# A three-stage kernel on one core: the filler's Silu made from tanh, and Silu's table loaded ahead

## The chip, the core and the metric

The kernel runs on one core of a Trainium2 chip. The metric is the device time of one execution in microseconds; less is better. A core has TensorE (matmuls, which read SBUF and write PSUM), ScalarE (activation functions from tables, copies), VectorE and GpSimd (elementwise work; GpSimd here works on SBUF only), and queues that start DMA transfers, here SyncE's. Each engine works through its own instructions in program order and waits for the others by semaphores. ScalarE has one table of functions active at a time; the profile shows a change of table as an instruction of its own, ACT_TABLE_LOAD.

## The reference

Three computations follow each other, all in float32. The notation below is the reference's, cut to what is computed:

```
scores = q @ k.T / 8 - slope[head] * distance      # causal, window of 128 keys, 576 tokens
x = softmax(scores) @ v                            # 4 batches x 8 heads, joined to x [2304, 512]
g = x @ w_gate                                     # [2304, 1536]
y = (g * sigmoid(g) * (x @ w_val)) @ w_out         # [2304, 512]
h = y @ w_in2                                      # [2304, 2048]
out = (h * cos(h)) @ w_out2                        # [2304, 512]
```

The product `g * sigmoid(g)` is Silu of g.

## The kernel before, in words

Every float32 matmul is made of three: each operand is split into a high part (rounded) and a low part (the rest), and high x high, high x low and low x high are summed in PSUM (`mm3`, lines 79 to 82). Much of the other engines' work is this splitting: a copy or cast to the high part, a subtraction for the low part.

**The attention phase** (lines 690 to 764) runs 144 items, nine for each of 16 pairs of batch and head pair. It is a software pipeline written out by hand: one turn `n` of the loop issues the scores of an item ahead, the bias (VectorE, line 540), Exp (ScalarE, line 549), the sum's reciprocal (VectorE, lines 555 and 560), the normalization (GpSimd, line 565), the transposes (TensorE, line 575), the copy of a transposed tile to its high part (ScalarE, line 592), the low part (VectorE, line 601), and the product with v (TensorE, line 638), each for an item some turns older than the one before. A list `post` carries work to the next turn: at its start a turn takes the whole list (line 703), and runs it behind its own issues and ahead of the filler (line 727). What a listed function appends to `post` runs one turn later. A second list, `pool_bg`, holds GpSimd work, of which each turn issues a bounded part.

**The filler.** TensorE's free time in that phase is filled with the second computation for the first three of its twelve column blocks (F0 = 3, 128 columns each). A generator (`filler`, line 284) walks over eight jobs, the two halves of 288 tokens of each of the four batches, as soon as the batch's attention is done. A job has 12 steps of the gate's matmuls (`a_l1` with "g": three column blocks by four parts of the inner dimension), then the 12 steps of the job before's second matmul (`a_l2`), then 12 steps of the value's matmuls (`a_l1` with "v"). Each step is one `mm3` of 288 columns. A turn adds 1.6 steps to what is due (RATE, lines 690, 696 and 730), and line 764 caps what may be carried over at the same 1.6, so that steps missed in a long wait are not made up within the phase. What is left of the filler runs after it (line 1037).

When a gate block is done, `evac_l1` (line 230) is called by way of `post`. It copies the block from PSUM to its third of the tile `fu` on ScalarE (line 234). With the third block it applies Silu to the whole tile of 128x864 (line 236) and sets a flag, `st["silu"]`. The filler holds the value's matmuls back until that flag is there (line 219):

```
while (nm, f) not in g0 or (nm == "v" and "silu" not in st):
    yield "wait"
```

The evacuation of a value block multiplies it with `fu` on VectorE (line 243); GpSimd then splits the product into `fh` and `fl` (lines 244 and 247), the operands of the second matmul. `fu` has one buffer, so the first copy of a job waits for the last `fl` of the job before.

**After the filler** line 1053 issues the first gate and value matmuls of the second computation's other blocks, and then the last job's second matmul (`a_l2`), whose four blocks VectorE and ScalarE evacuate in turn (lines 267 and 269). The rest of the second computation (`begin`, line 940) uses Silu at line 946, and the third, from about 640 us, uses Sin at line 1155 for the cosine, with VectorE's line 1152 in the chain before it. All these stages consist of matmuls in an order that is fixed in the program.

Of the kernel before, what the change touches and what calls it, by code (L numbers as in the profile page):

```python
# [9 lines left out]
F32 = mybir.dt.float32  # L10
F32R = mybir.dt.float32r
U32 = mybir.dt.uint32
AF = mybir.ActivationFunctionType
ALU = mybir.AluOpType
# [14 lines left out]
def kernel(  # L29
# [12 lines left out]
    nc = tc.nc  # L42
# [8 lines left out]
    HT = S // 2  # L51
# [8 lines left out]
    persist = ctx.enter_context(tc.tile_pool(name="persist", bufs=1))  # L60
    dram = ctx.enter_context(tc.tile_pool(name="dram", bufs=1, space=DRAM))
    halfpi = persist.tile([128, 1], F32, name="halfpi")
    xs, cv = ExitStack(), ExitStack()
    x_pool = xs.enter_context(tc.tile_pool(name="xhl", bufs=1, reuse_waits="tile"))
    wa2_p = ctx.enter_context(tc.tile_pool(name="wa2", bufs=3, side="right", reuse_waits="tile"))
# [10 lines left out]
    def f32(ap):  # L76
        return ap.bitcast(F32)

    def mm3(ps, ah, al, bh, bl, start, stop):
        nc.tensor.matmul(out=ps, lhsT=ah, rhs=bh, start=start, stop=False)  # L80
        nc.tensor.matmul(out=ps, lhsT=ah, rhs=bl, start=False, stop=False)  # L81
        nc.tensor.matmul(out=ps, lhsT=al, rhs=bh, start=False, stop=stop)  # L82
# [89 lines left out]
    post = deque()  # L172
# [10 lines left out]
    F0 = 3  # L183
    g0 = {}
    fa = ExitStack()
    pm = ctx.enter_context(tc.tile_pool(name="pm", bufs=2, space=PSUM, side="right"))
    fill_p = fa.enter_context(tc.tile_pool(name="fill", bufs=1, side="right"))
    ye_p = fa.enter_context(tc.tile_pool(name="ye", bufs=4, side="right"))

    g0_todo = []  # L190
    pools0 = [wa_p, wa_p, wa2_p]
# [5 lines left out]
    def flush():  # L197
        for _ in range(len(post)):
            post.popleft()()
# [9 lines left out]
    def bank():  # L209
        turn[0] += 1  # L210
        if more and turn[0] % 3 == 0:
            return more[0].tile([128, 512], F32, tag="l1", name="l1")
        return pm.tile([128, 512], F32, tag="pm", name="pm")

    def a_l1(job, nm, fs, st):
        b, hf = job
        tok = slice(b * S + hf * HT, b * S + (hf + 1) * HT)
        for f in fs:
            while (nm, f) not in g0 or (nm == "v" and "silu" not in st):
                yield "wait"  # L220
            ps = bank()
            wh, wl = g0[nm, f]
            for kk in range(KD):
                c = slice(kk * 128, (kk + 1) * 128)
                mm3(ps[:, :HT], wh[:, c], wl[:, c], xh[:, kk, tok], xl[:, kk, tok], kk == 0, kk == KD - 1)
                if kk == KD - 1:
                    post.append(lambda ps=ps, f=f: evac_l1(nm, f, st, ps))
                yield

    def evac_l1(nm, f, st, ps):  # L230
        if nm == "g":
            if f == 0:
                st["u"] = fill_p.tile([128, F0, HT], F32, tag="fu", name="fu")
            nc.scalar.copy(out=st["u"][:, f], in_=ps[:, :HT])
            if f == F0 - 1:
                nc.scalar.activation(out=st["u"], in_=st["u"], func=AF.Silu)
                st["silu"] = True
            return
        if f == 0:
            st["h"] = fill_p.tile([128, F0, HT], F32R, tag="fh", name="fh")  # L240
            st["l"] = fill_p.tile([128, F0, HT], F32R, tag="fl", name="fl")
        u, hi, lo = st["u"][:, f], st["h"][:, f], st["l"][:, f]
        nc.vector.tensor_tensor(out=u, in0=u, in1=ps[:, :HT], op=ALU.mult)  # L243
        pool_bg.append((0.35, lambda: nc.gpsimd.tensor_scalar(hi, u, 1.0, 0.0, ALU.mult, ALU.add)))

        def low():
            nc.gpsimd.tensor_tensor(out=lo, in0=u, in1=f32(hi), op=ALU.subtract)
            if f == F0 - 1:
                st["ready"] = True
        pool_bg.append((0.7, low))  # L250

    def a_l2(job, st):
        b, hf = job
        t0 = b * S + hf * HT
        while "ready" not in st or ("o", F0 - 1) not in g0:
            yield "wait"
        for e in range(KD):
            ps = bank()
            for f in range(F0):
                wh, wl = g0["o", f]  # L260
                c = slice(e * 128, (e + 1) * 128)
                mm3(ps[:, :HT], wh[:, c], wl[:, c], st["h"][:, f], st["l"][:, f], f == 0, f == F0 - 1)
                if f == F0 - 1:
                    def ev(ps=ps, e=e):
                        y = ye_p.tile([128, HT], F32, tag="ye", name="ye")
                        if e % 2:
                            nc.vector.tensor_copy(out=y, in_=ps[:, :HT])
                        else:
                            nc.scalar.copy(out=y, in_=ps[:, :HT])
                        nc.sync.dma_start(out=y1d[e, :, t0:t0 + HT], in_=y)  # L270
                    post.append(ev)
                yield
# [110 lines left out]
    for j in range(2):  # L383
        pair = []
        for nm in ("h", "l"):
            t = const.tile([128, 128], F32R, name=f"qt{nm}{j}")
# [3 lines left out]
        t = const.tile([128, 128], F32, name=f"qt{j}")  # L390
# [13 lines left out]
    for j in range(2):  # L404
        t = big.tile([128, NB, 4, D], F32, tag=f"vhl{j}", name=f"vx{j}")
# [289 lines left out]
    for n in range(N + PVS + 2):  # L695
        due += 0.7 * RATE
        u, idx = divmod(n, NI)
# [230 lines left out]
    def l1_mms(w, t0, n, ps=None):  # L928
        if ps is None:
            ps = bank()  # L930
        wh, wl = w
        tok = slice(t0, t0 + n)
        for kk in range(KD):
            c = slice(kk * 128, (kk + 1) * 128)
            mm3(ps[:, :n], wh[:, c], wl[:, c], xh[:, kk, tok], xl[:, kk, tok], kk == 0, kk == KD - 1)
        return ps[:, :n]
# [114 lines left out]
    load_acc(0)  # L1051
    i, tb, f = steps[0]
    early = [l1_mms(weights[i, nm, f], *tbs[tb], pl2.tile([128, 512], F32, tag="l2", name="l2")) for nm in ("v", "g")]
    for _ in a_l2(*last[0]):
        flush()
    flush()
# [22 lines left out]
    for k in range(K + 1):  # L1079
        if k < K:  # L1080
            i, tb, f = steps[k]
# [34 lines left out]
    def new_bank(n):  # L1116

        if n < 12 and n % 3:
            return pl2.tile([128, 512], F32, tag="l2", name="l2")
        return pm.tile([128, 512], F32, tag="pm", name="pm")  # L1120
# [118 lines left out]
    for k in range(K2 + 2):  # L1239
# [3 lines left out]
        for m in range(7):  # L1243
            if k < K2:
                if k == 0 and m < 2:
                    ps = bank0[m]
                elif m == 6:
                    prod(k, m, p7, start=False)
                    ps = p7
                else:  # L1250
                    ps = new_bank(7 * k + m)
# [57 lines left out]
```

## Time and profile before

| | us |
|---|---|
| median of 3 runs | 1018.39 |
| lowest and highest run | 1017.4, 1020.55 |
| the profiled execution, its own time | 1020.49 |
| its span, first to last instruction | 1018.3 |
| mean granted clock of TensorE, as a share of 2.4 GHz | 0.988 |
| attention phase with filler, without its thin start | 84 to 250 us of the span |
| the filler's rest | 250 to 300 us |

The profile lists for each engine the time in which it was busy. A group of instructions is named by its line, engine, operation and tiles (written <- read); then come the count, the busy time in us, the mean of one in ns, and the idle time of the engine just before them with what ended it. TensorE's matmuls are pipelined, so that the duration of one is longer than the distance of two starts.

### The profile page before, as it was taken

How to read it: one execution, taken by the hardware profiler on the slowest of the kernel's cores; microseconds unless marked ns; L12 is line 12 of the kernel's file. 1: busy time of each engine (PE TensorE's matmuls, PEld its weight loads, DVE VectorE, ACT ScalarE, POOL GpSimd, SP SyncE). 2: the span in 40 equal slices, each digit the busy share in tenths (PEclk: the TensorE clock that was granted, in tenths of full speed). 3: DMA queues.
4: the chain of work that ended last, by engine and by line, in shares of the span. 5: the costliest groups of instructions: out<-in, count | busy, mean ns of one | idle time of the engine just before them, and what ended most of it. 6: DMA issues, size and time to landing. Idle time of an engine off the chain costs nothing.

```text
span 1018.3 us, 17545 instructions
## 1 busy us (share of the span) xinstructions
PE 977.8 (96%) x5796; PEld 914.2 (90%) x5796; DVE 758.4 (74%) x1588; ACT 637.2 (63%) x1426; POOL 506.7 (50%) x575
## 2 busy tenths in 40 slices
PE   5779999999999999999999999999999999999998
PEld 3558999889999999999999999888999998989986
DVE  5996787776419898998989945789766797656664
ACT  5887888877215454555555532787767777677663
POOL 4775576665315666866867850234323343222231
PEclk9888999999999999999999999999999999999999
DMA  6551243212256454755846651856758566575552
GB/s 155 135 130 37 61 104 83 74 45 69 65 177 222 137 184 128 248 162 162 267 125 203 217 168 71 327 181 196 235 189 261 163 197 201 166 259 175 184 184 82
DMA packets 145161, 163.67 MB, mean 161 GB/s; under 512 B 64688, under 2 KB 105648, under 8 KB 144816
## 3 DMA queue, kind: packets, MB, share of 16 engines
q1 hardware_dynamic: 145072, 162.57, 51.4%
q8 instruction: 46, 0.75, 0.3%
q14 instruction: 43, 0.35, 0.1%
HBM read 126.88 MB, written 35.65 MB: 160 GB/s over the span
## 4 chain that ended last, share of the span: by engine, by line
PE 83%; ACT 7%; DVE 5%; issue 2%; DMA 2%; SPq 1%; POOL 0%; ACTq 0%; DVEq 0%; POOLq 0%
PE l L80 13%; PE l L81 13%; PE l L82 13%; PE pm L80 7%; PE pm L82 7%; PE pm L81 7%; PE pm L1033 5%; PE pm L1034 5%; PE pm L1035 5%; PE s L532 3%; PE t L575 2%; PE pv L638 2%; DVE e L540 1%; DVE ct L125 1%; PE pq L417 1%
## 5 line engine op out<-in xcount | busy, mean ns | idle before, releaser
L1157 POOL TENSOR_TENSOR r<-r,c 128x384 f32<-128x384 f32 x96 | 104.3, 1088 | 260.2 <-ACT r L1155 167.5
L80 PE MATMUL pm<-xh,wh 128*128 128x384 f32 (+1 forms) x452 | 152.3, 337 | 0.4 <-DVE fu L243 0.4
L82 PE MATMUL pm<-xh,wl 128*128 128x384 f32 (+1 forms) x452 | 145.9, 323 | 0.0
L81 PE MATMUL pm<-xl,wh 128*128 128x384 f32 (+1 forms) x452 | 145.9, 323 | 0.0
L81 PE MATMUL l<-wo,hh 128*128 128x512 f32 x288 | 113.1, 393 | 0.0
L80 PE MATMUL l<-wo,hh 128*128 128x512 f32 x288 | 113.0, 393 | 0.0
L82 PE MATMUL l<-wo,hl 128*128 128x512 f32 x288 | 112.9, 392 | 0.0
L854 POOL TENSOR_TENSOR cs<-cs,st 128x512 uint32<-128x512 uint32 x56 | 80.4, 1436 | 57.5 <-DVE cs L852 49.2
L1033 PE MATMUL pm<-xh,ws 128*128 128x384 f32 x318 | 107.4, 338 | 0.6 <-ACT q L1183 0.6
L1035 PE MATMUL pm<-xh,ws 128*128 128x384 f32 x318 | 107.1, 337 | 0.0
L1034 PE MATMUL pm<-xl,ws 128*128 128x384 f32 x318 | 107.1, 337 | 0.0
L565 POOL TENSOR_SCALAR e<-e,st 128x256 f32<-128x256 f32 (+1 forms) x144 | 67.0, 475 | 71.3 <-DVE st L560 27.1
L80 PEld LDWEIGHTS pm<-xh,wh 128*128 128x128 f32 x452 | 86.1, 190 | 1.9 <-DVE fu L243 0.7
L81 PEld LDWEIGHTS pm<-xl,wh 128*128 128x128 f32 x452 | 86.0, 190 | 0.0
L82 PEld LDWEIGHTS pm<-xh,wl 128*128 128x128 f32 x452 | 85.8, 190 | 0.0
L1147 ACT ACTIVATE a<-c 128x384 f32<-128x384 f32 x96 | 49.7, 518 | 53.6 <-DVE c L1173 53.6
L1152 DVE SCALAR_TENSOR_TENSOR r<-a,r 128x384 f32<-128x384 f32 x96 | 76.1, 793 | 3.3
L1154 ACT ACTIVATE r<-r 128x384 f32<-128x384 f32 x96 | 50.3, 524 | 41.7 <-DVE r L1152 41.7
L80 PE MATMUL l<-uh,wh 128*128 128x384 f32 x216 | 72.8, 337 | 0.0
L82 PE MATMUL l<-uh,wl 128*128 128x384 f32 x216 | 72.7, 337 | 0.0
L81 PE MATMUL l<-ul,wh 128*128 128x384 f32 x216 | 72.7, 336 | 0.0
L955 ACT CAST uh<-s 128x384 fp32r<-128x384 f32 x54 | 27.7, 514 | 69.9 <-PE l L82 62.2
(196 smaller groups left out, 2863.4 us busy)
## 6 DMA issues: line engine op xcount, KB each, us to landing
ws<-wid SPq DMA_DIRECT2D x168, 256.0 KB, 2.8
wo<-wod SPq DMA_DIRECT2D x48, 512.0 KB, 4.8
st<-in_moe_w_out_dram SPq DMA_DIRECT2D x28, 512.0 KB, 3.7
st<-in_moe_w_in_dram SPq DMA_DIRECT2D x16, 512.0 KB, 3.8
st<-in_moe_w_gate_dram SPq DMA_DIRECT2D x12, 512.0 KB, 4.2
st<-in_moe_w_val_dram SPq DMA_DIRECT2D x12, 512.0 KB, 3.7
wid<-sh SPq DMA_DIRECT2D x24, 256.0 KB, 4.0
wid<-sl SPq DMA_DIRECT2D x24, 256.0 KB, 3.6
```

Source lines behind the costliest of these rows:

```text
L80: nc.tensor.matmul(out=ps, lhsT=ah, rhs=bh, start=start, stop=False)
L81: nc.tensor.matmul(out=ps, lhsT=ah, rhs=bl, start=False, stop=False)
L82: nc.tensor.matmul(out=ps, lhsT=al, rhs=bh, start=False, stop=stop)
L565: nc.gpsimd.tensor_scalar(e[:, :w], e[:, :w], st[:, 6 + m:7 + m], 1.0, ALU.mult, ALU.mult)
L854: nc.gpsimd.tensor_tensor(out=ti, in0=ti, in1=st[:, :, 0], op=ALU.add)
L1033: nc.tensor.matmul(out=o, lhsT=wh, rhs=xh_, start=start and kk == 0, stop=False, skip_group_check=True)
L1034: nc.tensor.matmul(out=o, lhsT=wh, rhs=xl_, start=False, stop=False, skip_group_check=True)
L1035: nc.tensor.matmul(out=o, lhsT=wl, rhs=xh_, start=False, stop=kk == 1, skip_group_check=True)
L1147: nc.scalar.activation(out=a, in_=h, func=AF.Copy, scale=INV2PI, bias=MAGIC)
L1152: nc.vector.scalar_tensor_tensor(out=r, in0=a, scalar=-C2, in1=r, op0=ALU.mult, op1=ALU.add)
L1154: nc.scalar.activation(out=r, in_=r, func=AF.Abs)
L1157: nc.gpsimd.tensor_tensor(out=r, in0=r, in1=h, op=ALU.mult)
```

## The change

In the filler the gate's Silu is made in another way. With u = g / 2, g * sigmoid(g) = (tanh(u) + 1) * u. For each gate block ScalarE copies the bank with a scale of 0.5 into `fu`; one turn later it makes tanh of that into a new tile `th` (two buffers); one turn after the tanh VectorE makes (t + 1) * u in place, in one scalar_tensor_tensor. The flag is set with the third block's last operation. Besides, a Silu of one column into a tile that nobody reads stands behind the first matmuls of the next stage, ahead of the last job's second matmul.

```diff
@@ -60,6 +60,7 @@
     halfpi = persist.tile([128, 1], F32, name="halfpi")
+    gone = persist.tile([128, 1], F32, name="gone")
@@ -186,6 +187,7 @@
     ye_p = fa.enter_context(tc.tile_pool(name="ye", bufs=4, side="right"))
+    th_p = fa.enter_context(tc.tile_pool(name="th", bufs=2, side="right"))
@@ -231,10 +233,17 @@
         if nm == "g":
             if f == 0:
                 st["u"] = fill_p.tile([128, F0, HT], F32, tag="fu", name="fu")
-            nc.scalar.copy(out=st["u"][:, f], in_=ps[:, :HT])
-            if f == F0 - 1:
-                nc.scalar.activation(out=st["u"], in_=st["u"], func=AF.Silu)
-                st["silu"] = True
+
+            u = st["u"][:, f]
+            nc.scalar.activation(out=u, in_=ps[:, :HT], func=AF.Copy, scale=0.5)
+            t = th_p.tile([128, HT], F32, tag="th", name="th")
+            post.append(lambda: nc.scalar.activation(out=t, in_=u, func=AF.Tanh))
+
+            def gate():
+                nc.vector.scalar_tensor_tensor(out=u, in0=t, scalar=1.0, in1=u, op0=ALU.add, op1=ALU.mult)
+                if f == F0 - 1:
+                    st["silu"] = True
+            post.append(lambda: post.append(gate))
             return
@@ -1051,6 +1060,7 @@
     early = [l1_mms(weights[i, nm, f], *tbs[tb], pl2.tile([128, 512], F32, tag="l2", name="l2")) for nm in ("v", "g")]
+    nc.scalar.activation(out=gone, in_=halfpi, func=AF.Silu)
     for _ in a_l2(*last[0]):
```

## Rows read from the trace of the kernel before

**Rows 1.** The page: busy us of each engine, share of the span, instructions.

```profile
PE 977.8 (96%) x5796; PEld 914.2 (90%) x5796; DVE 758.4 (74%) x1588; ACT 637.2 (63%) x1426; POOL 506.7 (50%) x575
```

**Rows 2.** Busy times by stage; columns us, busy us (instructions) by engine, PEclk, DMA.

```profile
84.00:250.00 166.00, 156.15 (x1285) 147.18 (x1285) 124.26 (x461) 134.85 (x383) 108.05 (x207) 0.98 0.29 72
250.00:300.00 50.00, 49.81 (x364) 49.36 (x363) 16.03 (x31) 14.06 (x27) 11.80 (x18) 1.00 0.27 90
```

**Rows 3.** Groups of ScalarE instructions, whole span.

```profile
L1155 ACT ACTIVATE r<-r,halfpi 128x384 f32<-128x384 f32 x96 | 59.3, 618 | 3.1
...
L946 ACT ACTIVATE s<-pm 128x384 f32<-128x384 f32 x35 | 17.2, 492 | 49.1 <-PE pm L82 49.1
...
L234 ACT COPY fu<-pm 128x288 f32<-128x288 f32 x22 | 8.6, 395 | 13.7 <-POOL fl L247 11.0 <-PE pm L82 2.7
...
L236 ACT ACT_TABLE_LOAD x6 | 7.7, 1283 | 0.1
L236 ACT ACTIVATE fu<-fu 128x864 f32<-128x864 f32 x8 | 7.4, 926 | 0.1
...
L549 ACT ACT_TABLE_LOAD x5 | 6.4, 1283 | 0.1
...
L678 ACT ACT_TABLE_LOAD x1 | 1.3, 1283 | 0.7 <-PEq L1293 0.7
```

**Rows 4.** Timeline of ScalarE, first half's Silu; columns start us, duration us.

```profile
88.65 1.28 ACT L236 ACT_TABLE_LOAD   x1
89.95 0.93 ACT L236 ACTIVATE fu<-fu 128x864 f32<-128x864 f32 x1
90.89 1.28 ACT L549 ACT_TABLE_LOAD   x1
```

**Rows 5.** Busy times by stage, five stretches around the pairs of table loads.

```profile
88.00:100.00 12.00, 9.90 (x75) 8.72 (x74) 7.73 (x28) 10.64 (x26) 6.02 (x12) 0.86 0.15 33
114.00:124.00 10.00, 8.53 (x72) 8.08 (x72) 6.30 (x21) 9.84 (x26) 4.04 (x9) 1.00 0.05 16
150.00:158.00 8.00, 7.13 (x63) 6.44 (x63) 4.09 (x18) 7.70 (x18) 4.44 (x9) 1.00 0.16 37
186.00:198.00 12.00, 9.59 (x79) 8.68 (x78) 6.71 (x24) 11.12 (x27) 3.85 (x9) 1.00 0.37 89
224.00:232.00 8.00, 6.60 (x58) 5.97 (x56) 4.46 (x19) 7.88 (x20) 4.61 (x10) 1.00 0.20 52
```

**Rows 6.** Timeline of TensorE; in brackets idle us before, and its releaser.

```profile
93.22 0.29 PE L81 MATMUL pm<-xl,wh 128*128 128x288 f32 x1
93.35 0.29 PE L82 MATMUL pm<-xh,wl 128*128 128x288 f32 x1
95.30 0.63 PE L417 MATMUL pq<-ident,q 128*128 128x128 f32 x4 [1.65 <-issue]
...
197.14 0.40 PE L80 MATMUL pm<-fh,wh 128*128 128x288 f32 x1 [0.89 <-DVE ye L267]
```

**Rows 7.** Busy times by stage, behind the first stretch.

```profile
96.00:104.00 8.00, 7.56 (x40) 6.82 (x41) 5.63 (x21) 3.66 (x12) 6.96 (x13) 0.57 0.06 14
```

**Rows 8.** Groups of ScalarE instructions by form, 75 to 300 us.

```profile
L549 ACT ACTIVATE e<-e,st 128x256 f32<-128x256 f32 x66 | 33.1, 503 | 0.3
...
L592 ACT CAST pth<-t 128x512 fp32r<-128x512 f32 x24 | 14.0, 583 | 9.8 <-PE t L575 9.6
...
L592 ACT CAST pth<-t 128x384 fp32r<-128x384 f32 x22 | 10.5, 477 | 0.3
```

**Rows 9.** Groups of VectorE instructions by form, and line 1152 with min/median/max.

```profile
L1152 DVE SCALAR_TENSOR_TENSOR r<-a,r 128x384 f32<-128x384 f32 x96 | 76.1, 793 | 3.3
...
L243 DVE TENSOR_TENSOR fu<-fu,pm 128x288 f32<-128x288 f32 x21 | 9.3, 441 | 4.7 <-PE pm L82 4.7
...
L1152 DVE SCALAR_TENSOR_TENSOR r<-a,r x96: 557/558/2243, 641.1 to 1000.5; 128x384 f32<-128x384 f32 x96
```

## The prediction

> **What bounds the kernel now.** I began with busy time by engine [rows 1]: TensorE is busy 96% of the span, ScalarE 63%. The times of single stages then show where TensorE is not the limit. From 84 to 250 us, where attention runs with the first layer's matmuls as filler, it is busy 156.15 of 166 us, so 9.85 us are idle; from 250 to 300 us, where only the filler's rest runs, the idle time is 0.19 of 50 us [rows 2]. The order of the work is fixed in each queue, and the filler's rest is matmul work without gaps, so an idle microsecond taken out before 250 us brings all the rest forward by one.
>
> The groups of ScalarE instructions show why the change aims there [rows 3]: line 236 (Silu of the filler's gate) has 6 table loads of 1283 ns, line 549 (Exp) has 5. The first five halves each load Silu's table and then Exp's again; the sixth loads only Silu's, since no Exp follows; halves seven and eight load nothing. In time order the first half reads: load, Silu of 0.93 us, load, with about 0.02 us between them [rows 4]. Five stretches around those load pairs, 50 us in all, hold 8.25 us of TensorE's 9.85 us of idle: 2.10, 1.47, 0.87, 2.41 and 1.40 [rows 5]. ScalarE is busy 47.18 of the 50 us there, so it is the limit in them, while VectorE has 20.71 us free. The largest gap is 1.65 us long and ends at 95.30 us; a gap of 0.89 us ending at 197.14 us waits for VectorE's copy of the second matmul's bank [rows 6]. At the end of the first stretch the granted clock falls: it is 0.57 on average from 96 to 104 us [rows 7], so 0.43 x 8 / 0.5 = 6.9 of the 8 us are at the lower level, 1.2 GHz.
>
> **What goes.** Eleven loads of 1.283 us leave the attention phase, 14.1 us of ScalarE. This needs Tanh to be in the table that Exp leaves loaded, and no row shows a Tanh. The Trainium skill, page "ScalarE: Activation LUTs", section "Table sets: the hidden batching unit", lists tanh in the set of exp, by which all eleven go; no trace here has shown it yet. What the rows show is that one table serves several functions: Sin at line 1155 follows Silu at line 946 without a load of its own, and the only other load is the first, at line 678 [rows 3]. That section's neighbour, "What ACT_TABLE_LOAD costs", charges each switch 2.66 us with a drain; here a load takes 1.28 us and its neighbours touch it [rows 4], so I use the row.
>
> **What each half gains on ScalarE.** Before: three copies of 0.395, one Silu of 0.926 and two loads of 1.283, together 4.68 us [rows 3]. After: three scaled copies and three Tanh. The casts of 512 and 384 columns, 583 and 477 ns, give 0.83 ns a column [rows 8]. The ACTIVATE of line 946, from PSUM on 384 columns, takes 492 ns [rows 3]; less 96 columns that is 0.41 us, against 0.395 for the plain copy. I take 0.41, because a scaled copy is an ACTIVATE too. For Tanh on 128x288, Silu's 926 ns for 864 columns less 576 columns is 0.45 us, and Exp's 503 ns for 256 columns plus 32 is 0.53 us [rows 3, 8]. I take the middle, 0.49. Sum: 3 x 0.41 + 3 x 0.49 = 2.70 us, a relief of 1.98 us for each of halves one to five. Half six gains 0.69 us, halves seven and eight lose 0.59 us each, all after 250 us, where ScalarE is busy 14.06 of 50 us and covers it [rows 2]. Without that cover it would be 0.6 us each.
>
> **What of it reaches the path.** In each stretch no more than the smaller of the idle time and the relief can come back: 1.98, 1.47, 0.87 and 1.40 in stretches one, two, three and five. In the fourth I leave out the 0.89 us gap that waits for VectorE [rows 6], so 2.41 - 0.89 = 1.52. Together 7.24 us.
>
> **What is added.** *The later flag.* Each evacuation, Tanh, deferral and gate passes through the list that is emptied once a turn, so the gate is done three turns after the matmul instead of one. Line 219 holds back the value matmuls until then. For halves two to eight, twelve steps of the second matmul stand between, which cover two turns of 1.6 steps; without them every half would pay. The first half has no such steps: two turns without filler, 2 x 1.6 steps x 3 matmuls x 0.13 us (the spacing of starts [rows 6]) = 1.25 us that must be done later. Nothing if the first step is late anyway; 1.25 us at most; I take 1.25.
>
> *VectorE.* 24 gate operations, 18 before 250 us. The form is a scalar_tensor_tensor on two SBUF operands of 128x288; the nearest row is line 1152 on 384 columns, median 558 ns, mean 793 ns, longest 2243 ns [rows 9]. Line 243's tensor_tensor on the same 288 columns takes 441 ns, 117 less than that median. So a gate is 0.44 us undisturbed and 793 - 117 = 676 ns by the mean, and eighteen are 7.9 to 12.2 us. VectorE is free for 41.7 us between 84 and 250 us [rows 2], which hides them: cost 0, and up to 12.2 us if that cover is gone. Behind a waiting gate stand the next turn's bias and subtractions, then the scores' banks and TensorE. The gate's Tanh was issued a turn earlier, so the wait should be rare. The Trainium skill, "Advanced Engine Details and Errata", section "VectorE Performance Modes", says GpSimd and VectorE's two-port operations block each other through a shared port; by it the upper end would hold, and the spread of that row would fit it. Either end stays below the free time.
>
> *The rest.* The value product on VectorE waits for the gate instead of Silu, and GpSimd's splits wait for that product, 12 filler steps after the gate in every half but the first: nothing. The two th buffers are read a turn after being written and their third use comes two matmul groups later: nothing, and a turn if not. Banks are released by the scaled copy as by the copy. No DMA is added on any queue. The advance load of Silu, 1.28 us plus a tiny activation, stands on ScalarE just before the filler's last four evacuations, when the engine is mostly idle [rows 2]: nothing; at most 1.5 us if a bank waits for it.
>
> **The sum.** -7.24 + 1.25 = -5.99 us. The profiled execution took 1020.49 us (span 1018.3), so it would become 1014.5 us; it lies 2.1 us over the median of the runs, 1018.39, and from the median the forecast is 1012.4 us. I leave the clock's fall out of the sum: the first half keeps a thin spell for TensorE, idle before, unfilled after.
>
> **The rivals.**
> 1. *The clock stays up in the first half.* 6.9 us at the lower level do half the work [rows 7], so 3.4 us come on top: -9.4 us, 1009.0 us. For it: the idle gap before the fall shrinks. Against it: the two unfilled turns.
> 2. *The idle moves to another wait.* The load pair only comes last in those stretches; chains through VectorE, GpSimd's normalization and two PSUM banks per kind stand right behind. If only a third of the 7.24 comes back, -2.4 + 1.25 = -1.2 us: 1017.2 us, no measurable change. For it: the gap at 197.14 us names VectorE as its releaser already [rows 6]. Against it: VectorE has 20.71 of the 50 us free in these stretches, and outside them only 1.6 us of TensorE are idle [rows 2, 5].
> 3. *VectorE becomes the bound, slower.* Each gate stands in the turn's chain and prolongs it: -7.24 + 1.25 + 12.2 = +6.2 us, 1024.6 us, or +1.9 us (1020.3) at the short duration. It decides once VectorE's free time in the fill stretch, 41.7 us, is used up or lies in the wrong turns. Against it: that is over three times what is added.
> 4. *The change does not do what it says:* Tanh needs a table of its own. Then up to 18 Tanh stand between Exps with two loads each, 46 us of loads in place of 14.1: up to 32 us slower, 1050 us. No row excludes it; against it stands that one table serves Silu and Sin without a load between [rows 3].
>
> **How the numbers follow.** Forecast 0.60, rival 1 0.12, rival 2 0.19, rival 3 0.05, rival 4 0.04. A measurement of this kernel can tell 0.3%, about 3.1 us. Forecast and rival 1 are faster by more: 0.72. Rival 2 is the same: 0.19; rivals 3 and 4, slower, 0.09; rival 3 at its short duration would lie inside the bound, a small part that I leave there. The range's low end takes all 8.25 us and the 3.4 us of clock less 1.25, -10.4 us: 1008.0. The high end covers rival 2 and the little that is left of the gain if VectorE gives some back: 1018.0.
>
> **What would show it.** Right: no table load at lines 236 and 549, one load of Silu near 290 us and one at the start; Tanh rows of 0.45 to 0.53 us; idle of TensorE in the attention part down from 9.85 us to 3 or 4; ScalarE's busy time 5 x 1.98 + 0.69 - 2 x 0.59 - 1.5 = 7.9 us lower; the stage of line 946 starting about 6 us earlier with unchanged length. Wrong: loads beside Tanh; gate rows near 0.7 us with TensorE waiting for scores' banks; gaps of TensorE of the same length but other releasers; more than one further stretch at the lower clock near 90 us.

## The result and the profile after

The median of three runs is 1009.94 us (1008.31 to 1010.24) against 1018.39 us before, a ratio of 0.9912 with a 95% interval from 0.9894 to 0.993: 8.45 us less. The forecast was 1012.4 us, 6 us less. The profiled execution has a span of 1008.1 us, 10.2 us less than the one of before.

The page, busy time by engine (as in [rows 1]):

```profile
PE 972.8 (96%) x5796; PEld 908.0 (90%) x5796; DVE 774.1 (77%) x1612; ACT 626.6 (62%) x1433; POOL 510.2 (51%) x575
```

ScalarE is busy 10.6 us less, VectorE 15.7 us more. The same groups of ScalarE's instructions as in [rows 3], whole span (count, then busy us and mean ns, then idle before):

```profile
L240 ACT ACTIVATE th<-fu 128x288 f32<-128x288 f32 x24 | 10.6, 442 | 0.3
...
L238 ACT ACTIVATE fu<-pm 128x288 f32<-128x288 f32 x22 | 8.9, 404 | 14.9 <-POOL fl L256 13.3 <-PE pm L83 1.4
...
L687 ACT ACT_TABLE_LOAD x1 | 1.3, 1283 | 0.7 <-PEq L1303 0.7
L1063 ACT ACT_TABLE_LOAD x1 | 1.3, 1283 | 0.0
```

Of twelve loads two are left: the one at the start, and Silu's, loaded ahead at line 1063, at 273.6 us. Neither the tanh (line 240), nor the scaled copy (line 238), nor Exp (now line 558) has one. That is what the Trainium skill, "ScalarE: Activation LUTs", "Table sets: the hidden batching unit", says of exp and tanh, and this trace agrees. A tanh takes 0.442 us and a scaled copy 0.404.

The two stages, which end ten microseconds earlier now (columns as in [rows 2]: length, busy us of TensorE, its weight loads, VectorE, ScalarE and GpSimd, granted clock, DMA share, GB/s):

```profile
84.00:240.00 156.00, 150.90 (x1280) 143.46 (x1279) 131.60 (x478) 122.14 (x382) 109.81 (x206) 1.00 0.31 76
240.00:290.00 50.00, 50.00 (x369) 50.00 (x368) 20.61 (x41) 15.68 (x34) 11.94 (x19) 1.00 0.28 90
```

TensorE is idle 5.10 us where it was 9.85. Its timeline no longer shows the large gaps of the five stretches in [rows 5]. These are the larger ones that are left (in brackets: idle us before, and its releaser); the pair at 142 and 145 us comes again at 211 and 214 us:

```profile
89.05 0.46 PE L618 MATMUL pq<-ptt,v 128*128 128x128 f32 x2 [0.84 <-DVE kl L452]
...
114.38 0.40 PE L81 MATMUL pm<-fh,wh 128*128 128x288 f32 x1 [0.31 <-ACT fu L238]
...
142.41 0.38 PE L647 MATMUL pv<-pth,vhl 128*128 128x256 f32 x1 [0.73 <-DVE x L658]
...
145.40 0.46 PE L618 MATMUL pq<-ptt,v 128*128 128x128 f32 x2 [1.03 <-DVE kl L452]
```

And the stretch behind the first half's gate, where the clock was at 0.57 [rows 7]:

```profile
96.00:104.00 8.00, 8.00 (x69) 7.87 (x70) 6.94 (x25) 6.17 (x21) 7.33 (x14) 1.00 0.33 74
```

It is at full clock. The gate on VectorE, as a group, and its shortest, median and longest duration in ns (compare [rows 9]):

```profile
L243 DVE SCALAR_TENSOR_TENSOR fu<-th,fu 128x288 f32<-128x288 f32 x24 | 14.0, 584 | 6.4 <-ACT th L240 5.8 <-issue 0.5
```

```profile
L243 DVE SCALAR_TENSOR_TENSOR fu<-th,fu x24: 437/459/1307, 81.3 to 270.5; 128x288 f32<-128x288 f32 x24
```

The mean of 584 ns lies between the prediction's two bounds, 0.44 and 0.68 us, but it is a mean of two kinds, and the timeline tells them apart. Eight gates began while a GpSimd instruction was running. They took 599 to 1307 ns, and each ended 0.30 to 0.32 us behind the end of that instruction, as here:

```profile
107.99 0.75 POOL L665 TENSOR_TENSOR xl<-x,xh 128x256 fp32r<-128x256 f32 x1
108.25 0.80 DVE L243 SCALAR_TENSOR_TENSOR fu<-th,fu 128x288 f32<-128x288 f32 x1
```

The sixteen others took 437 to 460 ns. Line 1152 in the kernel before has the same two kinds: 24 that began beside a running GpSimd instruction, 1251 to 2243 ns, each ending 0.41 to 0.42 us behind it, and 72 of 557 to 562 ns. The Trainium skill, "Advanced Engine Details and Errata", "VectorE Performance Modes", says that GpSimd and VectorE's two-port operations block each other through a shared port; whether this operation is one of them its list does not say. No run here varied GpSimd's work.

From the third Silu of the next stage to the end both executions take 711.1 us (307.2 to 1018.3 before, 297.0 to 1008.1 after). All of the difference lies ahead of it, 9.8 of the 10.2 us behind the first copy of a gate block.

### The profile page after: what moved, and what is told of

Its sections match the earlier page's. It is cut to its first block, busy times and chain, and to the rows that moved or that the text cites. A ratio compares the mean times of both kernels' runs of the same rounds, so it can differ in the third digit from the quotient of the medians.

```text
span 1008.1 us, 17575 instructions
## 1 busy us (share of the span) xinstructions
PE 972.8 (96%) x5796; PEld 908.0 (90%) x5796; DVE 774.1 (77%) x1612; ACT 626.6 (62%) x1433; POOL 510.2 (51%) x575
## 4 chain that ended last, share of the span: by engine, by line
PE 86%; DVE 6%; ACT 4%; issue 2%; DMA 1%; POOL 1%; SPq 0%; DVEq 0%; ACTq 0%; POOLq 0%
PE l L81 13%; PE l L83 13%; PE l L82 13%; PE pm L81 8%; PE pm L82 7%; PE pm L83 7%; PE pm L1042 5%; PE pm L1044 5%; PE pm L1043 5%; PE s L541 3%; PE t L584 2%; PE pv L647 2%; DVE e L549 1%; DVE ct L126 1%; PE pq L426 1%
## 5 line engine op out<-in xcount | busy, mean ns | idle before, releaser
L558 ACT ACTIVATE e<-e,st 128x256 f32<-128x256 f32 (+1 forms) x144 | 68.0, 476 | 5.9 <-DVE st L549 5.3
```

The source lines that it names most:

```text
L558: nc.scalar.activation(out=e[:, :w], in_=e[:, :w], func=AF.Exp, bias=st[:, m:m + 1], scale=-1.0, accum_out=st[:, 2 + m:3 + m])
```

## The experiments

Two theories were set against each other. *A:* the pairs of table loads starved TensorE, and without them the time comes back. *B:* what helps is the gate's new form, block by block and partly on VectorE, without the 0.93 us Silu at its end. Beside that stood the sizes of the prediction's smaller terms: the later flag, VectorE, the clock.

For all profiles one length is compared, from the first copy of a gate block to the third Silu of the next stage, since the start before it varies by some 2 us from one execution to the next, whatever the kernel. TensorE's idle time is that length less its busy time; "lower clock" is the time at the lower level in that length, from 80 us on.

| kernel | median us | ratio to before, interval | length us | idle us | lower clock us |
|---|---|---|---|---|---|
| before, first profile | 1018.39 | | 226.8 | 11.13 | 6.8 |
| before_a | 1018.12 | | 224.8 | 10.89 | 3.4 |
| before_b | 1016.12 | | 223.3 | 10.75 | 0 |
| before_c | 1016.15 | | 224.2 | 10.43 | 3.4 |
| after | 1009.94 | 0.9912, 0.9894 to 0.993 | 217.0 | 6.14 | 0 |
| control (the change again) | 1009.37 | 0.9924, 0.9905 to 0.9944 | 215.7 | 5.59 | 0 |
| loads_back | 1019.52 | 1.0019, 1.0007 to 1.003 | 226.8 | 12.51 | 3.4 |
| loads_first | 1010.24 | 0.992, 0.9897 to 0.9942 | 217.6 | 6.80 | 0 |
| loads_later | 1017.43 | 0.9994, 0.9982 to 1.0007 | 223.8 | 11.07 | 0 |
| tanh_alone | 1004.04 | 0.9876, 0.986 to 0.9891 | 211.7 | 2.47 | 0 |
| early_flag | 1006.02 | 0.9892, 0.9874 to 0.991 | 212.1 | 2.77 | 0 |
| double_gate | 1012.54 | 0.9948, 0.9929 to 0.9967 | 223.0 | 8.02 | 10.2 |
| two_fu_early | 1002.14 | 0.9841, 0.9819 to 0.9863 | 209.2 | 0.91 | 0 |
| two_fu_late | 1003.46 | 0.9861, 0.9844 to 0.9877 | 211.2 | 2.30 | 0 |

The kernel before had 1017.45 us beside the first four runs, 1017.68 beside the second four and 1017.42 beside the last. before_a, before_b and before_c have one time each.

### The change again

> The changed kernel itself, run beside the others so that they can be set against it on the same chip. Both theories: 1008 to 1011 us, TensorE idle 4 to 5 us between 76 and 250 us, no stretch at the lower clock after 80 us.

1009.37 us, 8.1 us below the kernel before on the same chip. TensorE's seven gaps over 0.2 us between 76 and 240 us are the same ones to 0.01 us, and the clock does not fall after 80 us.

### The loads back

```diff
-            post.append(lambda: nc.scalar.activation(out=t, in_=u, func=AF.Tanh))
+            if f == 0:
+                jobs[0] += 1
+            back = f == F0 - 1 and jobs[0] in (1, 2, 3, 4, 5)
+
+            def tanh():
+                nc.scalar.activation(out=t, in_=u, func=AF.Tanh)
+                if back:
+                    nc.scalar.activation(out=gone, in_=halfpi, func=AF.Silu)
+            post.append(tanh)
```

> The changed kernel with the load pairs put back and nothing else: behind the third tanh of each of the first five halves stands a Silu of one column into a tile that nobody reads, so ScalarE loads Silu's table (1.28 us) and, at the next Exp, Exp's (1.28 us). Theory A (the load pairs starved TensorE): the time goes back to 1016 to 1020 us, since ScalarE's work per half, 2.6 + 2.6 + 0.2 us, is above that of the kernel before, and TensorE shows gaps of 0.9 to 2.4 us behind each pair. Theory B (what helped is that the gate is made block by block and partly on VectorE, without the 0.93 us Silu behind the third block): the time stays within 2 us of the control.

1019.52 us, 10.15 us above the control: the whole gain and a little more. ScalarE's groups show what was put back, and TensorE's timeline its largest gaps:

```profile
L249 ACT ACT_TABLE_LOAD x5 | 6.4, 1283 | 0.1
L568 ACT ACT_TABLE_LOAD x5 | 6.4, 1283 | 0.1
```

```profile
95.98 0.38 PE L551 MATMUL s<-kh,qh 64*128 64x256 f32 x1 [1.03 <-DVE st L559]
...
123.19 0.40 PE L81 MATMUL pm<-fh,wh 128*128 128x288 f32 x1 [1.97 <-DVE ye L286]
...
196.57 0.40 PE L81 MATMUL pm<-fh,wh 128*128 128x288 f32 x1 [1.97 <-DVE ye L286]
```

The gate's form is that of the change here, and nothing of the gain is left. Theory B falls. Ten loads and five small Silu are 13.8 us of ScalarE; TensorE's idle time grows by 6.9 us, to 12.51.

### The loads back in some halves

The same edit with (1,) in place of (1, 2, 3, 4, 5), and with (2, 3, 4, 5).

> The changed kernel with the load pair put back in the first half alone. Theory A with the clock as part of the pair's price: TensorE's gap of about 2 us returns behind the pair, the clock falls to its lower level once between 90 and 105 us, and the time is 4 to 6 us above the control (2 us of gap and up to 3.4 us of clock). Theory A without the clock (the clock's phase is chance, or the fall needs more than this gap): 1 to 2 us above the control, no fall.

> The changed kernel with the load pairs put back in halves two to five alone. Theory A: the gaps of these halves return, 0.9 to 2.4 us each, about 5 us above the control together, without a fall of the clock. If the clock made most of the gain: no more than 2 us above the control.

The pair in the first half costs 0.9 us by the medians, 1.9 us by the length. Two gaps come back:

```profile
92.76 0.63 PE L436 MATMUL pq<-ident,q 128*128 128x128 f32 x4 [0.25 <-issue]
...
95.97 0.38 PE L551 MATMUL s<-kh,qh 64*128 64x256 f32 x1 [1.03 <-DVE st L559]
```

The clock does not fall in this execution. The four later pairs cost 8.1 us by the medians as by the length, 2.0 us for a pair on average, without any fall either. The prediction had given these four 5.26 us, the sum of 1.47, 0.87, 1.52 and 1.40. A pair with its small Silu is 2.77 us of ScalarE. What it costs differs by half: from the first gate copy of a half to that of the next, loads_later is 2.6, 1.8, 2.6 and 0.8 us longer than the control in halves two to five. The 1.8 us stand where the kernel before showed only 0.87 us of idle time on TensorE.

### Tanh alone

```diff
+    gone = persist.tile([128, 1], F32, name="gone")
...
-                nc.scalar.activation(out=st["u"], in_=st["u"], func=AF.Silu)
+                nc.scalar.activation(out=st["u"], in_=st["u"], func=AF.Tanh)
...
+    nc.scalar.activation(out=gone, in_=halfpi, func=AF.Silu)
     for _ in a_l2(*last[0]):
```

> The kernel before with one word changed, Tanh in place of Silu over the 864 columns, and with Silu's table loaded ahead as in the change; it computes tanh(g) instead of Silu(g) for the first three column blocks. So the loads go, and the gate on VectorE, the three small Tanh and the later flag do not come. Theory A: 1008 to 1011 us, at or up to 1.25 us below the control, because the later flag's cost is missing. Theory B: 1016 to 1018 us, as nothing is split.

1004.04 us: 13.4 us below the kernel before and 5.3 us below the control, more than either theory had. So the loads alone are worth 13.4 us here, and the rest of the change, the gate's new form and the later flag, costs some 5. This kernel computes tanh(g), which is not Silu of g, so it is a measure and no kernel to use; its Tanh over the whole tile takes 927 ns where Silu took 926. The two rows below are the compared length in before_b, the execution of before in which the clock did not fall, and in this kernel:

```profile
80.10:303.40 223.30, 212.55 (x1710) 202.80 (x1709) 145.09 (x509) 156.25 (x429) 123.91 (x230) 1.00 0.31 84
```

```profile
78.90:290.60 211.70, 209.23 (x1710) 201.83 (x1709) 146.54 (x509) 143.18 (x419) 123.55 (x229) 1.00 0.32 88
```

TensorE's idle time goes from 10.75 to 2.47 us, 8.3 us, but the length by 11.6. The other 3.3 us come out of its busy time, 212.55 against 209.23 us for the same 1710 matmul rows at the same clock: in before_b they stand wider apart without a gap that the profile counts as idle. Part of that is the way busy time is counted. In [rows 6] matmuls start 0.13 us apart, but the last one before the gap counts as busy for its whole 0.29 us, some 0.16 us more. Between 76 and 240 us before_b has eleven gaps over 0.2 us and tanh_alone three, so that by this estimate 1.3 of the 3.3 us belong to gaps as well.

By halves, again from the first gate copy of one to that of the next, before_b is longer than tanh_alone by 2.7, 2.0, 1.8, 2.8 and 1.8 us in the five halves with a pair of loads, and by 0.6 us in the sixth, which has one. The prediction had 1.98, 1.47, 0.87, 1.52 and 1.40 us for the five.

### The early flag

```diff
             def gate():
                 nc.vector.scalar_tensor_tensor(out=u, in0=t, scalar=1.0, in1=u, op0=ALU.add, op1=ALU.mult)
-                if f == F0 - 1:
-                    st["silu"] = True
             post.append(lambda: post.append(gate))
+            if f == F0 - 1:
+                st["silu"] = True
```

> The changed kernel with the flag that releases the value's matmuls set when the third block is evacuated, as in the kernel before, not when its gate is made. By the sum of the prediction the first half's two turns without filler cost 1.25 us: 1008.7 us if the control is at 1009.9. Rival: turns without filler are shorter, and the steps come later in a place with free time, so nothing: within 0.5 us of the control.

1006.02 us, 3.35 us below the control, where the prediction's term was 1.25. (The intervals of the two ratios overlap; the gaps settle it.) Between 76 and 240 us the control's larger gaps sum to 4.95 us and this kernel's to 2.07. What goes is the first half's gap of 0.84 us, one of the two pairs of 0.73 and 1.03 us, and one of the two gaps of 0.31 us. The pair that stays:

```profile
206.01 0.39 PE L647 MATMUL pv<-pth,vhl 128*128 128x256 f32 x1 [0.73 <-DVE x L658]
...
208.99 0.46 PE L618 MATMUL pq<-ptt,v 128*128 128x128 f32 x2 [1.03 <-DVE kl L452]
```

Where the pair comes from can be read in the changed kernel around its first one, at 142 us. ScalarE stands still for 2.90 us before a half's first gate copy, since `fu` is still read by the last split of the half before on GpSimd. Behind it stands the copy of a product with v (line 656), which VectorE adds to (line 658), and TensorE's next product with v waits for that sum. Then the gate stands on VectorE ahead of a subtraction (line 452) whose bank TensorE needs next:

```profile
140.55 0.41 ACT L238 ACTIVATE fu<-pm 128x288 f32<-128x288 f32 x1 [2.90 <-POOL fl L256]
140.99 0.58 ACT L656 COPY x<-pv 64x512 f32<-64x512 f32 x1
...
141.67 0.68 DVE L658 TENSOR_TENSOR x<-pv,x 64x512 f32<-64x512 f32 x1 [3.70 <-ACT x L656]
```

```profile
144.19 0.46 DVE L243 SCALAR_TENSOR_TENSOR fu<-th,fu 128x288 f32<-128x288 f32 x1
...
144.57 0.68 DVE L452 TENSOR_TENSOR kl<-pq,kh 128x512 fp32r<-128x512 f32 x1
```

With the late flag halves three and five run into that wait at its full 2.9 us, with the early one only half five (2.8 us). By the program the flag holds steps back in the first half alone, which moves the later halves against the attention's turns; no run set the flag for single halves.

### Two buffers of the gate's tile

The early flag, or the late one of the change, and:

```diff
+    fu_p = fa.enter_context(tc.tile_pool(name="fu", bufs=2, side="right"))
     ye_p = fa.enter_context(tc.tile_pool(name="ye", bufs=4, side="right"))
...
-                st["u"] = fill_p.tile([128, F0, HT], F32, tag="fu", name="fu")
+                st["u"] = fu_p.tile([128, F0, HT], F32, tag="fu", name="fu")
```

> The changed kernel with the early flag and with two buffers of the gate's tile instead of one, so that the first copy of a half no longer waits on ScalarE for GpSimd's last split of the half before (13.9 us of ScalarE's idle time in the changed kernel, four waits). If these waits make the gaps of TensorE that are left (0.73 and 1.03 us, twice or three times): 2 to 4 us below the early flag alone. If the waiting engine had nothing to do for TensorE: within 0.5 us of it.

> The changed kernel with two buffers of the gate's tile and the late flag as it is in the change. If the late flag costs the first half's gap (0.84 us) and, by shifting the halves, a second wait of ScalarE for GpSimd's last split (gaps of 0.73 and 1.03 us near 140 us): both pairs of such gaps go, 0.84 and 0.31 us of gaps are left, and the time is 1002.5 to 1003.5 us, about 1 us above the two buffers with the early flag. Rival (the flag costs its 3.35 us by the steps that it pushes out of the phase): about 3.4 us above the two buffers with the early flag, 1005.5 us.

1002.14 us with the early flag, 3.9 us below the early flag alone, and 1003.46 with the late one. The pairs of gaps are gone in both. With the early flag one gap over 0.2 us is left between 76 and 240 us:

```profile
178.32 0.40 PE L81 MATMUL pm<-fh,wh 128*128 128x288 f32 x1 [0.31 <-ACT fu L239]
```

With the late flag the first half's 0.83 us and twice 0.31 us are left. So the flag itself costs 1.3 us by the medians, what the prediction had for it (1.25), and 2.0 by the length; 0.83 us of it is the first half's gap. Its other 2 us in the change (3.35 less 1.3) came by way of the wait for GpSimd. Two buffers with the early flag beat both kernels, by 15.5 us the one before.

### A second operation for the gate

```diff
             def gate():
+                nc.vector.scalar_tensor_tensor(out=t, in0=t, scalar=0.0, in1=t, op0=ALU.mult, op1=ALU.add)
                 nc.vector.scalar_tensor_tensor(out=u, in0=t, scalar=1.0, in1=u, op0=ALU.add, op1=ALU.mult)
```

> The changed kernel with a second VectorE operation of the gate's form ahead of each gate (t x 0 + t, in place), 24 in all, 18 of them in the attention phase, about 0.46 us each. Free time on VectorE hides the gate: within 1 us of the control. Rival (VectorE is close to the bound, each operation in the turn's chain prolongs it): 18 x 0.46 = 8 us above the control.

1012.54 us, 3.2 us above the control: neither nothing nor 8 us. The group of the added operation, and three gaps where the control has 0.84, 1.03 and 1.02:

```profile
L243 DVE SCALAR_TENSOR_TENSOR th<-th 128x288 f32<-128x288 f32 x24 | 12.5, 521 | 4.6 <-ACT th L240 4.6
```

```profile
87.70 0.65 PE L619 MATMUL pq<-ptt,v 128*128 128x128 f32 x2 [1.67 <-DVE kl L453]
...
147.46 0.46 PE L619 MATMUL pq<-ptt,v 128*128 128x128 f32 x2 [1.64 <-DVE kl L453]
...
218.78 0.46 PE L619 MATMUL pq<-ptt,v 128*128 128x128 f32 x2 [1.65 <-DVE kl L453]
```

Each has grown by 0.6 to 0.8 us, together 2.1: in these turns the gate stands in front of the subtraction that frees TensorE's bank. No other gap between 76 and 240 us has grown. (The clock fell twice in this profile, which the medians need not share.) The change itself has such a price too: the gap of 1.03 us is 0.63 us in the kernel before and in tanh_alone, 0.4 us less. That is not VectorE's alone. The same turn in early_flag, and then in tanh_alone:

```profile
207.08 0.43 ACT L240 ACTIVATE th<-fu 128x288 f32<-128x288 f32 x1
207.41 0.56 ACT L451 CAST kh<-pq 128x512 fp32r<-128x512 f32 x1
...
207.79 0.46 DVE L243 SCALAR_TENSOR_TENSOR fu<-th,fu 128x288 f32<-128x288 f32 x1
...
208.16 0.68 DVE L452 TENSOR_TENSOR kl<-pq,kh 128x512 fp32r<-128x512 f32 x1
```

```profile
207.08 0.56 ACT L443 CAST kh<-pq 128x512 fp32r<-128x512 f32 x1
...
207.79 0.67 DVE L444 TENSOR_TENSOR kl<-pq,kh 128x512 fp32r<-128x512 f32 x1
```

The subtraction starts 0.37 us later behind the gate. But the cast that it reads ends 0.33 us later too, behind the block's Tanh on ScalarE, and would have held it until about 207.97 us.

### The kernel before, three more times

> The kernel before once more, for a second profiled execution of it. If the load pair of the first half makes the clock fall: one fall to the lower level within 15 us of the first half's Silu, as in the first profile (96.7 to 103.5 us), and a length of 226 to 228 us from the first gate copy to the first Silu of the next stage. If the fall there was chance: none there, and that length is 223 to 224 us.

> The kernel before, a third profiled execution: the same two outcomes as for the second.

> The kernel before, a fourth profiled execution: the same two outcomes as for the second.

TensorE's gap behind the first half's load pair is 1.65 us long in all four executions. The stretch around and behind it, and one around the fifth half, in before_a, before_b and before_c:

```profile
90.00:110.00 20.00, 17.90 (x137) 16.41 (x136) 16.19 (x60) 15.70 (x50) 14.59 (x28) 0.91 0.26 58
222.00:232.00 10.00, 8.34 (x68) 7.61 (x67) 6.55 (x26) 9.87 (x25) 6.11 (x12) 1.00 0.11 30
```

```profile
90.00:110.00 20.00, 17.89 (x150) 16.51 (x149) 15.37 (x60) 17.21 (x52) 14.58 (x28) 1.00 0.27 61
```

```profile
90.00:110.00 20.00, 17.90 (x153) 16.45 (x151) 16.72 (x65) 17.14 (x55) 15.86 (x30) 1.00 0.22 51
222.00:232.00 10.00, 8.59 (x59) 8.07 (x58) 6.70 (x26) 8.92 (x25) 5.84 (x12) 0.83 0.11 39
```

The granted clock from 90 to 110 us is 0.91, 1.00 and 1.00 (0.83 in the first profile), and from 222 to 232 us 0.83 in before_c: 6.8, 3.4, 0 and 3.4 us at the lower level, the last in another half. So whether the clock falls behind such a gap differs from one execution to the next. Neither of the two expected outcomes fits before_a, which fell for half the time of the first and has a length of 224.8 us. (The length that the expectations speak of ends at the third Silu, as in the table.) The six profiles without load pairs, the doubled gate's aside, have no fall after 80 us; the two with the pairs in some halves have none either, and loads_back has one. With half the work done at the lower level, before loses an estimated 13.6 / 4 / 2 = 1.7 us by it on average.

## Why the prediction was right, and where its terms were off

**The cause** was the one named: pairs of loads on ScalarE that left TensorE idle. Put back, they take the whole gain with them. The rival that Tanh has a table of its own is out, and so is VectorE as the bound.

**The loads' term, 7.24 us, was too small.** The step that failed is "in each stretch no more than the smaller of the idle time and the relief can come back". With the loads gone and nothing added, 13.4 us came back. By that rule it would have been 7.36 us, since the relief is then the two loads, 2.57 us, and the first stretch counts with its whole 2.10. Against the mean of the four executions of before, a length of 224.8 us with 10.80 us of idle, tanh_alone has 13.1 us less: 8.3 us of idle, 1.7 us of clock, and 3.1 us in which TensorE counted as busy while its matmuls were wider apart, of which an estimated 1.3 stand at the gaps themselves. The idle part was near, 7.24 for 8.3; the 0.89 us gap that was left out belonged to it, since it went too. The other two were not in the sum.

**The relief on ScalarE** was set at 1.98 us for a half with 0.49 and 0.41 us for a tanh and a scaled copy; they took 0.442 and 0.404, so it was 4.68 - 2.54 = 2.14 us. For the tanh the end worked out from Silu, 0.45 us, was the right one, and with it ScalarE's busy time fell by more than the 7.9 us expected.

**The later flag, 1.25 us, was near by itself and wrong in place**: 1.3 us with two buffers by the medians and 2.0 by the length, 3.35 us in the change, because the shift brings half three, beside half five, into the long wait for `fu`. The prediction had said of the value's product and GpSimd's splits "nothing". That wait is also why 5.10 us of idle are left, not the 3 or 4 that were expected. The pair of gaps at 142 us, 1.76 us, has no like in the third half of the kernel before; the one at 211 us stood there too, with 0.73 and 0.63 us. So far rival 2, the idle that moves to another wait, came true in part.

**VectorE, 0 us, was too small.** Free time on average did not hide a VectorE operation in the turns where it stands ahead of the subtraction that frees a bank; the 24 that double_gate adds cost 3.2 us together. What the first one costs is open. From early_flag to tanh_alone, which differ in the gate's whole form, the blocks of Tanh on ScalarE included, it is 2.0 us by the medians and 0.4 us by the length, and the runs do not part the two engines' shares. The upper bound of 676 ns for one gate came from a mean over line 1152's two kinds, and so from how often GpSimd is at work beside that line.

**The clock** was left out of the sum, and that it stays up was rival 1, with a chance of 0.12. It did stay up after 80 us in both profiles of the change, but rival 1's 3.4 us are an estimated 1.7 on average, because before does not always lose them. That rival's time of 1009.0 us lies nearer to the measured one than the forecast does; its other terms were as far off.

By the medians: -13.4 for the loads with their clock, +2.0 for the gate's form, +3.35 for the flag, which is -8.1 us. That this is what the control gained is no test of it, as each term is the step from one kernel to the next. The prediction had -7.24, 0 and +1.25. The loads were 6.2 us too small and what is added 4.1 us too small; of opposite sign, the two errors left the sum 2.1 us off. The saving was set at about half of what the runs showed and the cost at under a quarter, so that the forecast came so near by luck; the direction and the cause it had right.

## What to carry to other kernels

Where one engine's table switch sits in a pipeline whose engines wait for each other every turn, its price can be well above the idle time of the bounding engine beside it: here 1.8 to 2.8 us for a pair of 2.6 us when the pairs were taken out of the kernel before, 1.8 us where only 0.87 us of idle showed. It is no constant either: put back into the change, the last pair cost 0.8 us. A step made later in the program's order is to be followed to the next shared buffer, not only to its own gap. And before a computation is rewritten to keep a table, look whether an added operation, on either engine, stands ahead of something that frees a bank.

## What was not expected of the hardware

The same gap of 1.65 us on TensorE, in the same place of the same program, was followed by 6.8 us at 1.2 GHz in one execution, 3.4 us in another and none in two more. A single profile's fall of the clock is therefore no fixed term of a sum. Of the same matmuls at the same full clock TensorE's busy time was 3.3 us longer in one kernel than in another, without more work, an estimated 1.3 us of it by the gaps. And a scalar_tensor_tensor that began while a GpSimd instruction was running ended at a nearly fixed time behind that instruction, 0.30 to 0.32 us for 128x288 and 0.41 to 0.42 us for 128x384; the others took 437 to 460 and 557 to 562 ns.
